# First batch's keys and queries loaded at once, scores of three pairs ahead of the first turning, transfers of one tile sent together

## The chip, the cores and the metric

One NeuronCore of a Trainium2 chip runs the whole program. The metric is the device time of one execution in microseconds (us), lower is better; the time of a kernel is the median of its runs. One further execution is taken by the hardware profiler, and all rows below are of that one.

## The reference

Inputs are random: `q`, `k`, `v` are (4 batches, 8 heads, 576 positions, 64), `s` is (4, 8, 576). All in fp32.

```python
scores = q @ k.T / 8
cum = cumsum(maximum(s, 0))
bias = -(cum[:, None] - cum[None, :])
scores = where(causal, -1e9, scores + minimum(bias, 0))
attn = softmax(scores)              # per batch and head
x = (attn @ v), heads side by side  # (4 * 576, 512)
x = ((x @ w_a) * (x @ w_b)) @ w_out          # w_a, w_b: 512 x 1536
h = x @ w_in                                 # w_in: 512 x 2048
out = (maximum(h, 0) + alpha * minimum(h, 0)) @ w_out2
```

## The kernel before

The 2304 tokens are worked in four blocks of the feed-forward part (`sizes`: 512, 512, 512 and 768 tokens). Each weight product is made of three fp32r products, since inputs and weights are split into a high part and a remainder (`wh`, `wl`; `xh`, `xl`; `gh`, `gl`). Blocks 0 to 2 run `ffn`, block 3 runs `ffn_seven`, which saves one of eight products. Weights come as 64-bit numbers, 90 tiles of 512 KB; in block 0 (and partly in block 1) each is decoded (`decode`: ScalarE, then VectorE) and stored once as fp32 in `w_d`, from which the later blocks read. `prefetch` loads weight tiles up to `ahead` tiles in front of the one in use.

Attention is cut per batch into the first 512 positions (`QA`) and the last 64 (`QB`), and into four pairs of heads (`HP`). For a pair: `load_kq` and `load_v` load, `s01` and `s23` make the scores of four strips of 128 queries (`q_k` on TensorE, then `soften`: minimum on VectorE, exponential on ScalarE, scaling on VectorE or GpSimd). In batch 0 `turn` then turns the probabilities on TensorE (twenty 128 x 128 products a pair, evicted into `pts`) and `av` multiplies with the values. In later batches the turning is done by VectorE in 32 x 32 tiles and by a way out to memory and back (`turned`: `zt`, `zd`, then `pt` or `pb`). The last 64 queries of a batch have steps of their own, `s4` and `av_b`, which need the tile `pb` (one buffer) and their own load of values with the argument `u = 1`: six pieces, a memset of a part of the tile ahead of them.

Only batch 0's attention stands ahead of the feed-forward part (`first_attention`, the first stage). The attention of later batches is cut into steps (`attention` lists them), which are strewn into the feed-forward blocks: `plan[0]` (batch 1) into block 0, `plan[1]` (batch 2 and the last queries of batch 1, then the last queries of batch 0 alone) into block 1, and so on.

The order of instructions on every engine is written by a planner (`Order`) while the program is built: a chain of work is a generator which yields the engines it could use with a cost, the planner takes whichever starts first, and `run.pe` advances its clock. A transfer is `dma`: a fixed cost on SP's queue, a transfer time by size, and an assumed time to land (`run.landing`, from `LANDING`, longer after the first stage). A chain with several `yield from dma(...)` issues the second one only after the planned landing of the first. `Slots` are counters of free buffers. Engines run their queues in order, SP too: a transfer that waits holds all behind it.

`due` takes the next step when its share of the block has come; outside block 0 it first asks `possible`, and puts the step off while its lag is below `BEHIND` (4) steps. `possible` looks at `s01`, `s23`, `s4` and `two_av`; any other step, `av_b` among them, counts as possible.

In `first_attention` before, the keys of pairs 0 and 1 are asked for at the start, those of pair i + 2 in round i, out of three buffers `kq`; scores of pair i + 1 follow a round behind the turning of pair i - 1; weights begin in round 2 (`FROM_WEIGHTS`), with ten ahead.

At the end, `store` copies each of the six output tiles of block 3 through four buffers `t` and sends it by SP.

Of the kernel before, what the change touches and what calls it, by code (L numbers as in the profile page):

```python
# [9 lines left out]
F32 = mybir.dt.float32  # L10
# [11 lines left out]
P = 128  # L22
D = 64
# [41 lines left out]

FROM_WEIGHTS, AHEAD, FROM_LEAD, FROM_STEPS, STEPS = 2, 10, 3, 4, 3

# [144 lines left out]
def attention_two_moe_kernel(  # L212
# [102 lines left out]
    def dma(o, i):  # L315
        yield {"sp": 480}, 700
        nc.sync.dma_start(o, i)
        yield {"dma": prod(o.shape) / (180 if o.dtype == U16 else 90)}, run.landing

    def split(src, hi, lo, sbuf=True):  # L320
        yield from copy(hi, src, 0.52 if sbuf else 1.04)
        yield from sub(lo, src, f32(hi), sbuf)


    def split_by(src, hi, lo, by):
# [14 lines left out]

    xh, xl = (
        [xp.tile([P, KD, 512], F32R, name=f"x{j}{i}") for i in range(2)] for j in "hl"
    )
    ovh = xp.tile([P, KD, OV], F32R, name="ovh")
# [39 lines left out]
    def running_sums(s_sb):  # L384
        nc.vector.tensor_scalar(s_sb, s_sb, 0.0, 8.0, op0=ALU.max, op1=ALU.mult)
        nc.vector.tensor_tensor_scan(cum[:, 0:S], s_sb, s_sb, 0.0, op0=ALU.add, op1=ALU.max)
        nc.sync.dma_start(cum_d, cum[:, 0:S])
        nc.vector.tensor_copy(cum[:, S:S + QB], cum[:, QA:S])
# [30 lines left out]

    def leave(b, t, o):  # L420
        if t < QA // P:
            yield from dma(out[b * S + t * P:b * S + (t + 1) * P, :], o)
        else:
            ends = [(2 * t - 2 * QA // P + j + 1) * S for j in range(2)]
            halves = [
                run.spawn(dma(out[e - QB:e, :], o[j * QB:(j + 1) * QB]), run.t)
                for j, e in enumerate(ends)
            ]
            for half in halves:
                yield half  # L430
        run.give(of_t, run.t)

# [18 lines left out]
    def load_v(b, hp, u):  # L451
        c0 = 2 * hp * D
        got = []

        def chain():
            yield of_vb
            vr = raw.tile([P, 5, 2 * D], F32, name="vb", tag="vb", bufs=VB)
            got.append(vr)
            if b + u >= TURN:
                keys = v[b, 0:QA, c0:c0 + 2 * D].rearrange("(c j k) d -> j k c d", j=4, k=32)  # L460
                if u:
                    yield {"pool": 240}, SEEN
                    nc.gpsimd.memset(vr[:, 4, :], 0.0)
                for j in range(4):
                    yield from dma(vr[j::4, 0:4, :], keys[j])
                    if u and j < 2:
                        k0 = QA + 32 * j
                        yield from dma(vr[j::4, 4, :], v[b, k0:k0 + 32, c0:c0 + 2 * D])
                return
            yield from dma(  # L470
                vr[:, 0:4, :], v[b, 0:QA, c0:c0 + 2 * D].rearrange("(c p) d -> p c d", p=P)
            )
            if u:
                yield {"pool": 240}, SEEN
                nc.gpsimd.memset(vr[QB:P, 4, :], 0.0)
                yield from dma(vr[0:QB, 4, :], v[b, QA:S, c0:c0 + 2 * D])

        v_t[b, hp, u] = got, run.spawn(chain(), slack=SL_QK)
# [20 lines left out]
    def load_kq(b, hp, u):  # L499

        got = []

        def chain():
            if not u and b >= STACK:
                halves = [run.spawn(stack(b, 2 * hp + j, got), run.t) for j in range(2)]
                yield halves[0]
                yield halves[1]
                return
            yield of_kq
            kq = raw.tile([P, 2 * QA], F32, name="kq", tag="kq", bufs=KQ)  # L510
            got.append(kq)
            if u:
                yield from dma(kq[:, 0:S + P], kq_b[b, hp])
            else:
                for j in range(2):
                    own = slice(j * D, (j + 1) * D)
                    yield from dma(kq[own], kq_a[b, 2 * hp + j, own])

        kq_t[b, hp, u] = got, run.spawn(chain())

    def load_sums(b, h, u):

        got = []

        def chain():
            yield of_c1 if u else of_c0
            nk = S if u else QA
            cb = raw.tile([P, nk], F32, name=f"cb{u}", tag=f"cb{u}", bufs=2 if u else CB)
            got.append(cb)
            n = P // (u + 1)  # L530
            for j in range(u + 1):
                bh = b * H + (u + 1) * h + j
                yield from dma(
                    cb[j * n:(j + 1) * n], cum_d[bh:bh + 1, 0:nk].to_broadcast([n, nk])
                )

        cb_t[b, h, u] = got, run.spawn(chain())

    def q_k(b, hp, r, dst):
# [30 lines left out]
        if r == 3:  # L570
            kq_t.pop((b, hp, 0))
            run.give(of_kq)

# [245 lines left out]

    def t4(b, hp, j):  # L820

        if j == 0:
            z_t[b, hp, 4] = probabilities(b, hp, 4)
        z = z_t[b, hp, 4]
        k, n = (QB, P) if j else (P, QA)
        at = slot()
        tp = banks[at][0:k, 0:n]
        for c in range(n // P):
            k0 = j * QA + c * P
            nc.tensor.transpose(tp[:, c * P:(c + 1) * P], z[:, k0:k0 + k], ident)  # L830
        run.pe(n / P * 107)
        if j:
            z_t.pop((b, hp, 4))
            run.give(of_z[4])

        def chain():
            if j == 0:
                yield of_pb
                pb_t[hp] = raw.tile([P, 5 * P], F32, name="pb", tag="pb")
                yield {"pool": 240}, SEEN  # L840
                nc.gpsimd.memset(pb_t[hp][QB:P, QA:5 * P], 0.0)
            o = j * QA
            yield from copy(pb_t[hp][0:k, o:o + n], tp, 1.04)

        e_t[b, hp, 4 + j] = read_by(at, chain())

    def av_b(b, hp):

        turned = b + 1 >= TURN
        if turned:  # L850
            settle((b, hp, 4))
        else:
            run.need(*(e_t.pop((b, hp, 4 + j)) for j in range(2)))
        got, ready = v_t.pop((b, hp, 1))
# [3 lines left out]
        pv = banks[at][:, 0:QB]  # L858
        for c in range(5 if turned else 0):
            for j in range(2):  # L860
# [3 lines left out]
                    p[:, 2 * j:2 * j + 2, c, :], start=c == 0, stop=c == 4,  # L864
                )
        for c in range(0 if turned else 5):
            for j in range(2):
                o = c * P + j * QB
                nc.tensor.matmul(
                    pv[64 * j:64 * j + 64], got[0][:, c, j * D:(j + 1) * D], pb[:, o:o + QB],  # L870
                    start=c == 0, stop=c == 4,
                )
# [13 lines left out]
    def first_attention():  # L886
# [6 lines left out]
        run.now = 2000.0  # L893
        run.pump()
        running_sums(s_sb)
        run.now = 5000.0
        for rs in ((0, 1), (2,)):
            both(0, 0, rs)
        for i in range(HP + 2):
            if i + 2 < HP:  # L900
                load_kq(0, i + 2, 0)
            if i < HP:
                load_v(0, i, 0)
                both(0, i, (3,))
                s01(0, i)
                if i + 1 < HP:
                    both(0, i + 1, (0, 1))
            if 0 <= i - 2:
                av(0, i - 2)
            if i < HP:  # L910
                s23(0, i, 2)
                if i + 1 < HP:
                    both(0, i + 1, (2,))
                s23(0, i, 3)
            if i == FROM_WEIGHTS:
                nc.sync.dma_start(alpha_sb, alpha)
                ahead = AHEAD
                prefetch()
            if i == FROM_LEAD:
                for f, args in plan[0][0]:  # L920
                    f(*args)
            if 0 <= i - 1 < HP:
                for c in range(3):
                    for j in range(2):
                        turn(0, 2 * (i - 1) + j, c)
            if i >= FROM_STEPS:
                for f, args in plan[0][1][:STEPS]:
                    f(*args)
                del plan[0][1][:STEPS]

# [303 lines left out]
    def possible(f, args):  # L1234
        rings = 1 if f == two_av else 2
        if f not in (s01, s23, s4, two_av):
            return True
        if not seen(*(reader[i] for i in ring[:rings] if i in reader)):
            return False
        if f == two_av:  # L1240
# [4 lines left out]
            )  # L1245
        b, hp = args[:2]
        if f == s4:
            return seen(kq_t[b, hp, 1][1], z_t[b, hp, 4][1])
# [170 lines left out]
    def ffn_seven(blk, sums):  # L1419
# [334 lines left out]
    def ffn(blk):  # L1754
# [57 lines left out]
        def store(t):  # L1812
            yield of_t
            o = ft.tile([P, DM], F32, name="o", tag="t")
            yield from copy(o, acc[t], 1.04, SHRUNK ** 2)
            run.spawn(leave(blk, t, o), run.t)

# [142 lines left out]
```

## Time and profile before

| | us |
|---|---|
| median of 3 runs | 991.97 |
| runs | 991.25 to 992.36 |
| the profiled execution: its time | 991.26 |
| the profiled execution: span from first to last instruction | 989.5 |

The profile shows one execution. A timeline row gives the start, the time of the (merged) instructions, engine, source line and operation, the number of instructions, and in brackets how long the engine had stood idle and who released it. A line is often that of a helper: L317 is `dma`, L292 `dve`, L276 `act`, L284 a copy by ScalarE. PE is TensorE, PEld its weight load, DVE VectorE, ACT ScalarE, POOL GpSimd, SPq the queue of SP. Matmuls overlap, so the distance of their starts, not their length, is their pace. PEclk is the granted clock of TensorE: 1.00 is 2.4 GHz, 0.50 is 1.2 GHz.

### The profile page before, as it was taken

The numbers are of one execution on the slowest core, as the hardware profiler recorded it, in microseconds if no ns is written. First come the engines' busy times: TensorE is split into PE (matmuls) and PEld (weight loads), VectorE is DVE, ScalarE is ACT, GpSimd is POOL, SyncE is SP. The second block draws the span as 40 slices with busy tenths as digits, with TensorE's granted clock in tenths as the row PEclk, the third lists the DMA queues.
The fourth block names the chain that finished last, engine by engine and source line by source line (L and its number), as shares of the span: only waits on it lengthen the run. The fifth ranks groups of instructions, "written<-read, shape, count | busy, mean of one in ns | idle before, by whom it ended". The sixth has DMA issues, their size and how long they took to land.

```text
span 989.5 us, 15862 instructions
## 1 busy us (share of the span) xinstructions
PE 964.1 (97%) x5235; PEld 811.8 (82%) x5235; DVE 745.3 (75%) x1725; ACT 559.3 (57%) x1162; POOL 231.9 (23%) x291
## 2 busy tenths in 40 slices
PE   6999999999999999969999999999999999999997
PEld 5577777788888888858888888888899999999896
DVE  7897878868788878847578868666497888788772
ACT  6976767657665657526455547544552333566443
POOL 2130113321155556303235434522100000000000
PEclk9999999999999999979999999999999999999999
DMA  7589997789599978977498786855403223021202
GB/s 191 179 283 320 344 364 248 280 291 320 202 285 297 319 247 280 283 222 231 151 273 252 214 273 195 252 177 176 161 24 105 65 64 103 27 65 65 64 0 65
DMA packets 140115, 196.78 MB, mean 199 GB/s; under 512 B 35776, under 2 KB 79808, under 8 KB 140032
## 3 DMA queue, kind: packets, MB, share of 16 engines
q1 hardware_dynamic: 130240, 177.93, 57.5%
q10 hardware_dynamic: 9792, 17.83, 4.9%
q8 instruction: 41, 0.67, 0.3%
q14 instruction: 42, 0.34, 0.1%
HBM read 152.13 MB, written 43.59 MB: 198 GB/s over the span
## 4 chain that ended last, share of the span: by engine, by line
PE 94%; DVE 2%; DMA 2%; ACT 2%; issue 0%; SPq 0%; ACTq 0%
PE bank L1223 21%; PE bank L1224 21%; PE bank L1225 21%; PE bank L1854 5%; PE bank L1856 4%; PE bank L1855 4%; PE bank L804 3%; PE bank L1707 2%; PE bank L1706 2%; PE bank L1708 2%; PE bank L547 2%; PE bank L744 1%; PE bank L566 1%; PE bank L862 1%; DMA kq<-in_kq_a_dram 1%; ACT z L276 1%
## 5 line engine op out<-in xcount | busy, mean ns | idle before, releaser
L1223 PE MATMUL bank<-xh,wh 128*128 128x512 f32 (+1 forms) x620 | 237.8, 384 | 0.0
L1224 PE MATMUL bank<-xl,wh 128*128 128x512 f32 (+1 forms) x620 | 234.3, 378 | 0.9 <-DVE xl L292 0.9
L1225 PE MATMUL bank<-xh,wl 128*128 128x512 f32 (+1 forms) x620 | 234.1, 378 | 0.0
L284 ACT ACTIVATE wh<-raw 128x512 fp32r<-128x512 f32 (+1 forms) x198 | 115.0, 592 | 91.8 <-PE bank L1224 39.0
L1223 PEld LDWEIGHTS bank<-xh,wh 128*128 128x128 f32 x620 | 116.5, 188 | 25.7 <-issue 6.5
L1224 PEld LDWEIGHTS bank<-xl,wh 128*128 128x128 f32 x620 | 116.6, 188 | 19.9 <-DVE xl L292 1.4
L1225 PEld LDWEIGHTS bank<-xh,wl 128*128 128x128 f32 x620 | 116.5, 188 | 19.4
L301 POOL TENSOR_TENSOR wl<-raw,wh 128x512 fp32r<-128x512 f32 x68 | 92.1, 1359 | 114.7 <-ACT wh L284 82.8
L301 DVE TENSOR_TENSOR wl<-raw,wh 128x512 fp32r<-128x512 f32 (+1 forms) x136 | 84.4, 633 | 39.9 <-ACT wh L284 33.6
L276 ACT ACTIVATE z<-z,mn 128x512 f32<-128x512 f32 (+4 forms) x144 | 83.0, 578 | 36.9 <-DVE mn L292 36.2
L1223 PE MATMUL bank<-gh,wh 128*128 128x512 f32 (+1 forms) x240 | 89.6, 373 | 0.0
L1224 PE MATMUL bank<-gl,wh 128*128 128x512 f32 (+1 forms) x240 | 88.6, 369 | 0.0
L1225 PE MATMUL bank<-gh,wl 128*128 128x512 f32 (+1 forms) x240 | 88.4, 368 | 0.0
L1854 PE MATMUL bank<-wh,gh 128*128 128x512 f32 x192 | 77.8, 405 | 0.0
L284 ACT ACTIVATE gh<-g 128x512 fp32r<-128x512 f32 x84 | 52.8, 628 | 43.1 <-DVE g L292 42.8
L1856 PE MATMUL bank<-wh,gl 128*128 128x512 f32 x192 | 75.5, 393 | 0.0
L1855 PE MATMUL bank<-wl,gh 128*128 128x512 f32 x192 | 75.5, 393 | 0.0
L1004 ACT ACTIVATE top<-raw 128x512 f16<-128x512 bf16 x90 | 69.2, 785 | 7.1 <-DMA raw<-in_w_dram 3.8
L301 DVE TENSOR_TENSOR gl<-g,gh 128x512 fp32r<-128x512 f32 x68 | 51.6, 759 | 18.4 <-ACT gh L284 17.5
L301 POOL TENSOR_TENSOR wl<-w,wh 128x512 fp32r<-128x512 f32 x24 | 31.8, 1323 | 134.8 <-ACT wh L284 92.0
L311 DVE TENSOR_SCALAR z<-z,sm 128x512 f32<-128x512 f32 (+4 forms) x103 | 59.0, 597 | 1.3
L292 DVE STREAM_TRANSPOSE zt<-z 128x384 f32<-128x384 f32 (+2 forms) x88 | 56.2, 650 | 4.8 <-DMA zd<-zt 3.8
(149 smaller groups left out, 1915.0 us busy)
## 6 DMA issues: line engine op xcount, KB each, us to landing
raw<-w_d SPq DMA_DIRECT2D x91, 512.0 KB, 4.3
raw<-in_w_dram SPq DMA_DIRECT2D x90, 512.0 KB, 5.9
w_d<-w ACTq DMA_DIRECT2D x46, 256.0 KB, 5.7
zd<-zt SPq DMA_DIRECT2D x48, 192.0 KB, 4.7
pt<-zd SPq DMA_DIRECT2D x48, 192.0 KB, 5.6
kq<-in_kq_a_dram SPq DMA_DIRECT2D x16, 512.0 KB, 6.1
vb<-in_v_dram SPq DMA_DIRECT2D x112, 64.0 KB, 4.4
zd<-zt SPq DMA_DIRECT2D x24, 256.0 KB, 2.9
```

What stands on the lines that cost most here:

```text
L276: nc.scalar.activation(o, i, func, **k)
L284: nc.scalar.activation(o, i, AF.Copy, scale=by)
L292: f(*args, **k)
L301: (nc.gpsimd if eng == "pool" else nc.vector).tensor_tensor(o, i0, i1, op=ALU.subtract)
L311: (nc.gpsimd if eng == "pool" else nc.vector).tensor_scalar(o, i, s0, s1, op0=ALU.mult, op1=ALU.mult)
L1004: nc.scalar.activation(top.bitcast(F16).rearrange("p (n t) -> p n t", t=2)[:, :, 1], r.bitcast(BF16)[:, 4:4 + 4 * WN].rearrange("p (n t) - ...
L1223: nc.tensor.matmul(o, wh, ih, start=first, stop=False)
L1224: nc.tensor.matmul(o, wh, il, start=False, stop=False)
L1225: nc.tensor.matmul(o, wl, ih, start=False, stop=last)
L1854: nc.tensor.matmul(acc[t], gh[:, c], wh, start=first, stop=False)
L1855: nc.tensor.matmul(acc[t], gh[:, c], wl, start=False, stop=False)
L1856: nc.tensor.matmul(acc[t], gl[:, c], wh, start=False, stop=last)
```

## The change

1. Keys and queries of batch 0 go into two tiles of two pairs each (`kq_0`), in the memory that the second block's `x` has later; all four pairs are asked for at the start, and their values too. Batch 0 takes none of the three `kq` buffers.
2. Two weight tiles (`EARLY_TILES`) are asked for between the keys of pairs 1 and 2; ten ahead from the scores of pair 1 on.
3. The order of the first stage is written out: scores of pairs 0, 1 and 2, turning of 0, scores of 3, then turnings and products with values in turn. The load for batch 1 (`lead`) comes after the scores of pair 1. The store of `cum_d` moves from the running sums to behind the scores of pair 0.
4. `dmas` starts several transfers of one tile at once, where a chain issued one behind the other: values of later batches (four or six pieces), halves of keys, the two halves of `cb`, and rows of the output.
5. `possible` knows `av_b`: it waits until the planner sees `pb` and the values.
6. In block 3, the two output tiles which are made first take buffers `d`, and the last tile is copied and sent in two halves, by ScalarE on its own queue and by VectorE on SP's.
7. Code for a way of turning that no batch takes (`t4`, branches in `av_b` and `load_v`) is removed.

```diff
-FROM_WEIGHTS, AHEAD, FROM_LEAD, FROM_STEPS, STEPS = 2, 10, 3, 4, 3
+AHEAD, EARLY_TILES, STEPS = 10, 2, 3
...
+    def dmas(*pairs):
+
+        sent = [run.spawn(dma(o, i), run.t) for o, i in pairs]
+        for c in sent:
+            yield c
...
-    xh, xl = (
-        [xp.tile([P, KD, 512], F32R, name=f"x{j}{i}") for i in range(2)] for j in "hl"
-    )
+    xh, xl = ([xp.tile([P, KD, 512], F32R, name=f"x{j}0")] for j in "hl")
+    kq_0 = [xp.tile([P, 2, 2 * QA], F32, name="kq", tag=f"x{j}1") for j in "hl"]
...
-        nc.sync.dma_start(cum_d, cum[:, 0:S])
...
+            if b + u < TURN:
+                yield from dma(
+                    vr[:, 0:4, :], v[b, 0:QA, c0:c0 + 2 * D].rearrange("(c p) d -> p c d", p=P)
+                )
                 return
-            yield from dma(
-                vr[:, 0:4, :], v[b, 0:QA, c0:c0 + 2 * D].rearrange("(c p) d -> p c d", p=P)
-            )
+            keys = v[b, 0:QA, c0:c0 + 2 * D].rearrange("(c j k) d -> j k c d", j=4, k=32)
+            pairs = [(vr[j::4, 0:4, :], keys[j]) for j in range(4)]
             if u:
                 yield {"pool": 240}, SEEN
-                nc.gpsimd.memset(vr[QB:P, 4, :], 0.0)
-                yield from dma(vr[0:QB, 4, :], v[b, QA:S, c0:c0 + 2 * D])
+                nc.gpsimd.memset(vr[:, 4, :], 0.0)
+                for j in range(2):
+                    k0 = QA + 32 * j
+                    pairs.append((vr[j::4, 4, :], v[b, k0:k0 + 32, c0:c0 + 2 * D]))
+            yield from dmas(*pairs)
...
-            yield of_kq
-            kq = raw.tile([P, 2 * QA], F32, name="kq", tag="kq", bufs=KQ)
+            if b or u:
+                yield of_kq
+                kq = raw.tile([P, 2 * QA], F32, name="kq", tag="kq", bufs=KQ)
+            else:
+                kq = kq_0[hp // 2][:, hp % 2]
             got.append(kq)
             if u:
                 yield from dma(kq[:, 0:S + P], kq_b[b, hp])
             else:
-                for j in range(2):
-                    own = slice(j * D, (j + 1) * D)
-                    yield from dma(kq[own], kq_a[b, 2 * hp + j, own])
+                own = [slice(j * D, (j + 1) * D) for j in range(2)]
+                yield from dmas(*((kq[o], kq_a[b, 2 * hp + j, o]) for j, o in enumerate(own)))
...
         run.now = 2000.0
         run.pump()
+        ahead = EARLY_TILES
+        prefetch()
+        run.now = 3000.0
+        run.pump()
+        for i in range(2, HP):
+            load_kq(0, i, 0)
+        for i in range(HP):
+            load_v(0, i, 0)
+        run.pump()
         running_sums(s_sb)
         run.now = 5000.0
...
+        scores(0)
+        nc.sync.dma_start(alpha_sb, alpha)
+        nc.sync.dma_start(cum_d, cum[0:BH, 0:S])
+        scores(1)
+        ahead = AHEAD
+        prefetch()
+        f, args = lead.pop(0)
+        f(*args)
+        scores(2)
+        turns(0)
+        scores(3)
+        for x, j in ((xh, "h"), (xl, "l")):
+            x.append(xp.tile([P, KD, 512], F32R, name=f"x{j}1", tag=f"x{j}1"))
+        for f, args in lead:
+            f(*args)
+        turns(1)
+        av(0, 0)
+        turns(2)
+        av(0, 1)
+        turns(3)
+        av(0, 2)
+        of_steps(STEPS)
+        av(0, 3)
+        of_steps(STEPS)
...
-        rings = 1 if f == two_av else 2
-        if f not in (s01, s23, s4, two_av):
+        rings = 1 if f in (two_av, av_b) else 2
+        if f not in (s01, s23, s4, two_av, av_b):
             return True
...
+        if f == av_b:
+            return (b, hp, 4) in e_t and seen(e_t[b, hp, 4], v_t[b, hp, 1][1])
...
         def store(t):
-            yield of_t
-            o = ft.tile([P, DM], F32, name="o", tag="t")
-            yield from copy(o, (acc + banks[0:2])[t], 1.04, SHRUNK ** 2)
-            run.spawn(leave(blk, t, o), run.t)
+            slots = of_t if t < QA // P else of_d
+            yield slots
+            if t < QA // P:
+                o = ft.tile([P, DM], F32, name="o", tag="t")
+            else:
+                o = pools["big"]([P, T], F32, "d", 5)[:, 0:DM]
+            src = (acc + banks[0:2])[t]
+            if t + 1 == QA // P:
+                for c in (slice(0, DM // 2), slice(DM // 2, DM)):
+                    run.spawn(last_half(t, o, src, c), run.t)
+                return
+            yield from copy(o, src, 1.04, SHRUNK ** 2)
+            run.spawn(leave(blk, t, o, slots), run.t)
+
+        def last_half(t, o, src, c):
+            by_act = c.start == 0
+            if by_act:
+                yield from act(o[:, c], src[:, c], AF.Copy, scale=SHRUNK ** 2)
+            else:
+                yield from dve(
+                    DM // 2, 1.04, nc.vector.tensor_scalar, o[:, c], src[:, c], SHRUNK ** 2, None,
+                    op0=ALU.mult,
+                )
+            rows = out[blk * S + t * P:blk * S + (t + 1) * P, c]
+            yield {"act" if by_act else "sp": 480}, 700
+            (nc.scalar if by_act else nc.sync).dma_start(rows, o[:, c])
```

In the new `first_attention`, `scores(i)` is `both` and then `s01`, `s23(2)`, `s23(3)` of pair i; `turns(i)` its six turnings; `of_steps(3)` the next three steps of `plan[0]`.

## Rows read from the trace of the kernel before

**Rows 1.** The page: busy us of each engine, its share of the span, instructions
```profile
...
PE 964.1 (97%) x5235; PEld 811.8 (82%) x5235; DVE 745.3 (75%) x1725; ACT 559.3 (57%) x1162; POOL 231.9 (23%) x291
...
```

**Rows 2.** Waits of TensorE: for whom, us in total, times, longest us
```profile
...
PE bank L862 <- DMA vb<-in_v_dram: 7.9, 1, 7.9
PE bank L399 <- DVE cum L386: 5.4, 1, 5.4
...
```

**Rows 3.** Busy us by stretch (columns: engines, granted clock, DMA share, GB/s)
```profile
...
0.00:54.34 54.34, 44.06 (x277) 30.31 (x277) 41.61 (x182) 42.94 (x129) 10.89 (x25) 0.97 0.67 185
...
62.00:190.00 128.00, 127.06 (x659) 100.28 (x659) 103.27 (x227) 88.03 (x167) 30.09 (x24) 1.00 0.92 314
...
```

**Rows 4.** Timeline of the start: start us, us, engine, line, operation
```profile
...
1.19 1.21 SPq L317 DMA_DIRECT2D kq<-in_kq_a_dram  x2
...
7.71 0.48 PE L560 MATMUL bank<-cums,rows 64*128 64x128 f32 x2
...
9.12 0.58 PE L566 MATMUL bank<-kq 64*128 64x128 f32 x1 [0.40 <-DMA kq<-in_kq_a_dram]
...
13.30 0.90 PE L560 MATMUL bank<-cums,rows 64*128 64x128 f32 x1
...
```

**Rows 5.** The chain that ended last, its start: start us, us, what
```profile
...
5.60 3.48 DMA kq<-in_kq_a_dram
...
```

**Rows 6.** Timeline of TensorE in the first stage
```profile
...
24.36 0.33 PE L560 MATMUL bank<-cums,rows 64*128 64x128 f32 x2
...
25.44 2.38 PE L811 MATMUL bank<-pt,vb 128*64 128x512 f32 x16
27.75 0.44 PE L560 MATMUL bank<-cums,rows 64*128 64x384 f32 x2
...
29.85 2.40 PE L771 MATMUL bank<-ident,z 128*128 128x128 f32 x20
...
```

**Rows 7.** Busy us by stretch of the first stage
```profile
...
0.00:7.70 7.70, 2.33 (x13) 2.31 (x13) 4.69 (x8) 4.87 (x20) 2.40 (x10) 1.00 0.47 110
...
17.13:24.36 7.23, 4.40 (x21) 3.80 (x20) 7.02 (x42) 6.58 (x21) 3.41 (x6) 0.76 1.05 311
...
30.00:38.00 8.00, 8.00 (x63) 5.24 (x63) 6.78 (x33) 8.00 (x25) 1.58 (x3) 1.00 0.00 0
...
```

**Rows 8.** Timeline of TensorE around the wait for values
```profile
...
416.50 0.80 PE L862 MATMUL bank<-pb,vb 128*64 128x64 f32 x20
...
434.66 1.33 PE L862 MATMUL bank<-pb,vb 128*64 128x64 f32 x20 [7.87 <-DMA vb<-in_v_dram]
...
440.68 0.39 PE L1225 MATMUL bank<-xh,wl 128*128 128x512 f32 x1
...
```

**Rows 9.** Busy us by stretch around the wait for values
```profile
...
436.00:438.00 2.00, 2.00 (x5) 1.62 (x6) 0.23 (x1) 0.23 (x1) 0.00 (x0) 0.50 0.34 79
...
```

**Rows 10.** Timeline of GpSimd and of SP in the same stretch
```profile
...
417.37 0.20 POOL L463 MEMSET vb<- 128x128 f32 x1 [2.17 <-PE bank L862]
...
424.12 0.58 SPq L317 DMA_DIRECT2D pb<-zd  x1
...
431.90 1.90 SPq L317 DMA_DIRECT2D vb<-in_v_dram  x3
...
```

**Rows 11.** Waits of SP from 405 to 436 us
```profile
...
SPq L317 <- DVE zt L292: 4.5, 2, 3.6
...
```

**Rows 12.** DMA issues from 400 to 436 us: KB each, median us to landing
```profile
...
vb<-in_v_dram SPq DMA_DIRECT2D x10, 64.0 KB, 4.4
...
pb<-zd SPq DMA_DIRECT2D x1, 320.0 KB, 5.5
...
```

**Rows 13.** Timeline of TensorE and of ScalarE at the end
```profile
...
982.77 0.39 PE L1708 MATMUL bank<-wh,gl 128*128 128x512 f32 x1
...
983.45 0.60 ACT L284 ACTIVATE o<-bank 128x512 f32<-128x512 f32 x1 [1.03 <-DMA out_dram<-o]
984.78 0.60 ACT L284 ACTIVATE o<-bank 128x512 f32<-128x512 f32 x1 [0.74 <-DMA out_dram<-o]
```

More of the change, by code (lines that the diff above doesn't have):

```diff
@@ L418, in attention_two_moe_kernel, with leave @@
     NB = len(sizes)
-    def leave(b, t, o):
+    def leave(b, t, o, slots):
         if t < QA // P:
@@ L424, in leave @@
             ends = [(2 * t - 2 * QA // P + j + 1) * S for j in range(2)]
[L425 to L431, printed above, removed]
+            yield from dmas(
+                *((out[e - QB:e, :], o[j * QB:(j + 1) * QB]) for j, e in enumerate(ends))
+            )
+        run.give(slots, run.t)
     pb_t, scores = {}, []
@@ L458, in chain @@
             got.append(vr)
[L459 to L468, printed above, removed]
+            if b + u < TURN:
+                yield from dma(
+                    vr[:, 0:4, :], v[b, 0:QA, c0:c0 + 2 * D].rearrange("(c p) d -> p c d", p=P)
+                )
                 return
-            yield from dma(
-                vr[:, 0:4, :], v[b, 0:QA, c0:c0 + 2 * D].rearrange("(c p) d -> p c d", p=P)
-            )
+            keys = v[b, 0:QA, c0:c0 + 2 * D].rearrange("(c j k) d -> j k c d", j=4, k=32)
+            pairs = [(vr[j::4, 0:4, :], keys[j]) for j in range(4)]
             if u:
                 yield {"pool": 240}, SEEN
-                nc.gpsimd.memset(vr[QB:P, 4, :], 0.0)
-                yield from dma(vr[0:QB, 4, :], v[b, QA:S, c0:c0 + 2 * D])
+                nc.gpsimd.memset(vr[:, 4, :], 0.0)
[3 more added lines that the diff above has]
+            yield from dmas(*pairs)
         v_t[b, hp, u] = got, run.spawn(chain(), slack=SL_QK)
@@ L530, in chain @@
             n = P // (u + 1)
[L531 to L534, printed above, removed]
-                )
+            yield from dmas(*(
+                (
+                    cb[j * n:(j + 1) * n],
+                    cum_d[bh:bh + 1, 0:nk].to_broadcast([n, nk]),
+                )
+                for j, bh in enumerate(range(b * H + (u + 1) * h, b * H + (u + 1) * (h + 1)))
+            ))
         cb_t[b, h, u] = got, run.spawn(chain())
@@ L571, in q_k @@
             kq_t.pop((b, hp, 0))
-            run.give(of_kq)
+            if b:
+                run.give(of_kq)
     def z_space(r, b, h):
@@ L818, in av @@
         x_done[b].append(read_by(at, split(pv, *parts, False)))
[L820 to L845, printed above, removed]
-    def av_b(b, hp):
[L849 to L853, printed above, removed]
+    def av_b(b, hp):
+        settle((b, hp, 4))
         got, ready = v_t.pop((b, hp, 1))
@@ L858, in av_b @@
         pv = banks[at][:, 0:QB]
-        for c in range(5 if turned else 0):
+        for c in range(5):
             for j in range(2):
@@ L864, in av_b @@
                     p[:, 2 * j:2 * j + 2, c, :], start=c == 0, stop=c == 4,
[L865 to L871, printed above, removed]
                 )
@@ L894, in first_attention @@
         run.pump()
+        ahead = EARLY_TILES
[7 more added lines that the diff above has]
+        run.pump()
         running_sums(s_sb)
         run.now = 5000.0
[L897 to L929, printed above, removed]
@@ new lines, in first_attention, with scores, turns, of_steps @@
+        lead, steps = plan[0]
+        def scores(i):
+            both(0, i, (0, 1))
+            both(0, i, (2,))
+            both(0, i, (3,))
+            s01(0, i)
+            s23(0, i, 2)
+            s23(0, i, 3)
+        def turns(i):
+            for c in range(3):
+                for j in range(2):
+                    turn(0, 2 * i + j, c)
+        def of_steps(n):
+            for f, args in steps[:n]:
+                f(*args)
+            del steps[:n]
+        scores(0)
+        nc.sync.dma_start(alpha_sb, alpha)
@@ new lines, in first_attention @@
+        nc.sync.dma_start(cum_d, cum[0:BH, 0:S])
[10 more added lines that the diff above has]
+        for f, args in lead:
+            f(*args)
+        turns(1)
[4 more added lines that the diff above has]
+        av(0, 2)
@@ L1648, in store @@
         def store(t):
-            yield of_t
-            o = ft.tile([P, DM], F32, name="o", tag="t")
-            yield from copy(o, (acc + banks[0:2])[t], 1.04, SHRUNK ** 2)
-            run.spawn(leave(blk, t, o), run.t)
+            slots = of_t if t < QA // P else of_d
[19 more added lines that the diff above has]
+                    op0=ALU.mult,
+                )
+            rows = out[blk * S + t * P:blk * S + (t + 1) * P, c]
+            yield {"act" if by_act else "sp": 480}, 700
+            (nc.scalar if by_act else nc.sync).dma_start(rows, o[:, c])
         def x2_part(o, j, d, c):
@@ L1815, in store @@
             yield from copy(o, acc[t], 1.04, SHRUNK ** 2)
-            run.spawn(leave(blk, t, o), run.t)
+            run.spawn(leave(blk, t, o, of_t), run.t)
         for f in range(NF1 + 1):
```

## Prediction

> **What bounds the kernel now.** I read the page first: TensorE is busy for 964.1 of 989.5 us [rows 1], so a gain can come only from the 25 us in which it stands still, from time at a low clock, or from stretches where its pipeline crawls. Next the waits of TensorE: two carry most, 7.9 us in one wait for a load of values and 5.4 us before its first instruction [rows 2]. Then the table by stretches: in the first stage, up to the first feed-forward product at 54.34, TensorE is busy for 44.1 us, so 10.3 are idle; from 62 to 190 us only 0.9 are [rows 3]. There and in most of the rest TensorE is the bound, so an earlier arrival at 54.34 is passed on, if the weights follow. The change touches the first stage, the place of the 7.9 us, and the end; I price each.
>
> **The first stage, its head.** Two chains lead to the first scores. The sums of `s` let the first score product run at 7.71; the change leaves this chain as it is. The keys and queries of pair 0: SP issues two halves at 1.19, then stands at the store of `cum_d`, which needs the scan, and issues the next only at 5.60, 3.48 us before TensorE goes on with it at 9.12, after 0.40 us of waiting [rows 4, 5]. In the new code all halves of pairs 0 and 1 precede the store. Pair 0 should be there by 1.8 + 3.5 = 5.3, ahead of 7.71, which frees about 1.4 us at the head. The later keys (1 MB), two weight tiles (1 MB) and the values (1 MB) are also sent early. The rows show 185 to 314 GB/s [rows 3]; at an assumed 230, pair 2, behind 2.5 MB, lands near 2 + 11 = 13 us, and it is wanted after two pairs of scores, near 14.5. I charge nothing; at 185 GB/s it would come at 15.5 and cost 1 us, which the range holds.
>
> **The first stage, its end.** Two bounds. TensorE's work at full speed: a pair's scores 1.08 + 2.10 = 3.18 us (24.36 to 25.44, 27.75 to 29.85), its twenty turnings 2.40, its values product 2.31 [rows 6]. Five pairs of scores (batch 1's first lies in the stage) and four of the others: 15.9 + 9.6 + 9.2 = 34.7. Pair 0's own scores were 2.0 us slower than 3.18 (7.71 to 13.30, less 0.40 [rows 4]), which I keep. 7.71 + 34.7 + 2.0 = 44.4 us: TensorE cannot be through earlier, a gain of 9.9. The other bound is ScalarE and VectorE, which share minima, exponentials, scaling, eviction and the weights' parts. From 7.7 to 54.34 they are busy for 38.1 and 36.9 us, 75.0 together, in 93.3; in the fullest stretches for 14.8 of 16.0 (30 to 38) and 13.6 of 14.5 us (17.13 to 24.36), 93% [rows 3, 7]. With all of it done at that density from 9.7 on (two us after the first product, as some scores must be there), it takes 40.3 us: 50.0. Part of the 75 belongs to weight tiles which the first products don't need yet; how much, the rows don't say, so I go some way from 50.0 towards 44.4: 48.8, a gain of **5.5**. The ends are 0 and 9.9. The new order speaks for a fuller ScalarE, since three pairs' scores are ahead of the first turning: now it is idle for 46.6 - 38.1 = 8.5 us. The clock of 0.76 from 17.13 to 24.36, behind TensorE's own 2.8 us of idle time there, costs 1.7 us [rows 7]; that it goes is part of the 5.5.
>
> Weights: block 0 runs almost without waits, at 314 GB/s [rows 3]. Two tiles are now decoded before the crush, so the stock at 48.8 should not be smaller than it is at 54.34. I cost this at nothing; what hides a late tile is that stock, and if the supply does not follow, this part falls to nothing.
>
> **The stall at 426.8.** It is the first `av_b` of batch 0's tail. TensorE stands for 7.87 us until 434.66. Then the clock is 0.50: the twenty small products take 1.33 us, where the same took 0.80 at 416.50, and from their end, 435.99, to 440.68 half of 4.7 us is lost. Price: 7.87 + 0.53 + 2.35 = 10.7 us [rows 8, 9]. What came last is a load of values: its pieces are issued one after another, each after the planner's landing of the one before, and the last three stand on SP at 431.90, behind a transfer that waited up to 3.6 us for a transposition [rows 10, 11]. Two edits attack it. `dmas` sends the six pieces in a row after the memset at 417.37: 6 x 0.6 = 3.6 us of SP, and landed by 421.2 + 4.4 = 425.6, before the stall begins. Left is `pb`: issued at 424.12, 5.5 us to land, 429.6 [rows 10, 12]. And `possible` now postpones `av_b` until the planner sees both; the lag may grow to four steps, a few us each by the distance of such steps, where 2.8 us are wanted. With both, **10.7**; with the first alone 7.87 - 2.8 = 5.1. What the change queues behind six pieces in a row is whatever SP issues next, a weight tile, up to 3.6 us later. Tiles are taken up to ten ahead, and one lasts for twelve products; I cost it at nothing, and rival 3 is what happens if that cover is gone.
>
> **The end.** The last product starts at 982.77 and takes 0.39. ScalarE's last two copies wait 1.03 and 0.74 us for buffers of outputs that are still leaving; the last ends at 985.38, and 4.1 us later all is over [rows 13]. In the new code two of the tiles use other buffers, so no copy waits, and the last is halved over two engines: 983.16 + about 0.4 = 983.6, then two sends side by side. Gain 985.4 - 983.6 = **1.8** us, with 4.1 kept; 1.2 to 2.2 if the halves take more or less than I assume. The Trainium skill (DMA: Bandwidth & Descriptors, Anatomy of one DMA) gives a transfer a fixed part of about 2.0 us and a part by bytes. By this half the bytes would land some 0.3 us earlier, an estimate, and the end would give 2.1. No row shows half a tile, so the sum stays at 1.8.
>
> **Sum.** 991.26 (the profiled execution: span 989.5 and 1.8 around it) - 5.5 - 10.7 - 1.8 = 973.3. The median of the runs lies 0.7 above the profiled one: **974.0**. A difference under 0.2% (2 us) could not be told from none.
>
> **Rivals.**
> 1. *The first stage gives nothing* (0.17). ScalarE is full from 30 to 38 us [rows 7]; if the early decodings stand in its order ahead of exponentials while their loads are still coming, or VectorE holds TensorE at each reuse of a bank, the stage ends near 54 again. Against it: 10.3 us of idle TensorE there. 991.97 - 10.7 - 1.8 - 0.5 = 979. One cause that would bring this about shows in the rows: idle time of 2.8 us goes with clock 0.76. The Trainium skill (TensorE: Matmul & The Clock Gate, A second HAM failure mode) says that small idle times between groups of products throttle the clock again; by that, three pairs of scores paced by VectorE would bring the low clock back.
> 2. *Half of the stall stays* (0.13): the planner takes `av_b` at once, and it waits for `pb` until 429.6. 991.97 - 5.5 - 5.1 - 1.8 = 979.6.
> 3. *Slower* (0.05): loads of values in a row on SP hold up the weights. There are 28 such loads, of four or six pieces. From 18.0 / 28 = 0.65 us of delay in each that comes through to TensorE, all is eaten; with 1 us it is 991.97 - 18.0 + 28 = 1002. Against it: 0.9 us of idle time in 128 [rows 3], so there is stock.
> 4. *TensorE bounds the first stage* (0.07): it ends at 44 to 45 us, and the time is 969.6.
>
> The forecast has 0.58, with 971 to 977. Half the stall and nothing from the first stage together give 984.6, about the upper end; the lower is the TensorE bound with the larger gain at the end, 969.2. Range **968 to 984**. Faster 0.93 (all but rival 3 and mishaps that add up), same 0.02, slower 0.05.
>
> **What would show it.** The first score product at 7.7 with no wait for keys after it; the first feed-forward product at 47 to 51; clock 1.00 from 17 to 25; no wait of TensorE over 1 us at the first lone `av_b` and clock 1.00 behind it; the last copy ending within 0.6 us of the last product. I am wrong if the first feed-forward product comes after 53, if a new wait of several us stands in blocks 0 to 2, or if TensorE waits for weights.

## The result, and the profile after

The changed kernel takes 996.96 us (median; 994.48 to 999.8) beside 991.9 us for the kernel before on the same chip: ratio 1.0052, 95% interval 1.0038 to 1.0065. It is slower by half a per cent, where I forecast 974.0 and gave slower a chance of 0.05.

The page of the changed kernel shows the span first; TensorE's busy time is that of [rows 1] to 0.1 us, so in sum the 3.1 us between the two spans are idle time of TensorE. The profiled execution, 994.48, is the fastest of the seven: 3.2 us of the 5.1 between the medians stand in the traces, the other 1.9 in none.

```profile
span 992.6 us, 15863 instructions
...
PE 964.0 (97%) x5235; PEld 810.5 (82%) x5235; DVE 739.1 (74%) x1711; ACT 560.5 (56%) x1169; POOL 236.5 (24%) x299
```

Its waits of TensorE (for whom, us in total, times, longest us) answer to [rows 2]:

```profile
PE bank L403 <- DVE cum L391: 5.4, 1, 5.4
PE bank L833 <- DMA pb<-zd: 5.0, 1, 5.0
PE bank L548 <- DVE mn L292: 3.0, 2, 1.9
PE bank L773 <- POOL z L311: 2.5, 4, 1.3
PE bank L806 <- DMA pt<-zd: 2.4, 2, 2.0
PE bank L548 <- DVE xl L301: 1.7, 1, 1.7
```

The 7.9 us for values are gone, and in their place stand waits for `pb`, for `pt` and for scores. Where they stand is read from the windows. The first two lines answer to [rows 3], the others bracket batch 0's tail, where [rows 8, 9] had the wait:

```profile
0.00:50.54 50.54, 41.05 (x277) 28.30 (x277) 40.85 (x178) 41.46 (x126) 12.22 (x26) 0.97 0.72 200
58.25:186.25 128.00, 127.05 (x659) 100.24 (x659) 102.15 (x228) 87.44 (x166) 30.74 (x24) 1.00 0.91 310
...
350.00:430.00 80.00, 72.23 (x445) 57.89 (x444) 56.66 (x133) 41.57 (x87) 34.51 (x46) 0.98 0.80 247
430.00:437.00 7.00, 7.00 (x48) 5.58 (x47) 5.49 (x12) 3.67 (x8) 1.38 (x2) 1.00 0.90 305
437.00:500.00 63.00, 57.96 (x294) 47.05 (x293) 36.49 (x68) 29.63 (x56) 14.44 (x20) 0.95 0.60 195
```

I set every feed-forward product of one trace against the same product of the other and read the lag (after minus before). It is -3.8 us at the first (50.54 instead of 54.34) and stays there for 300 us. From about 355 to 425 us it rises by 12.2 to +8.4. At the old stall it falls by 11.5 to -3.1. Between 465 and 474 it rises by 6.8 to +3.6, and the last product is 4.1 us late. Behind it 1.0 comes back, so the span is 3.1 us longer. The three gains of the forecast are there (3.8, 11.5 and 1.0 us); two losses in block 1, 12.2 and 6.8 us, eat them.

**The second loss, in full.** TensorE stands for `pb` and then runs at 0.50 of its clock, the lower of its two levels (its timeline, then the windows):

```profile
469.77 1.34 PE L833 MATMUL bank<-pb,vb 128*64 128x64 f32 x20 [5.04 <-DMA pb<-zd]
```

```profile
469.70:474.00 4.30, 4.23 (x27) 3.57 (x28) 1.57 (x3) 0.22 (x1) 0.00 (x0) 0.50 1.02 350
```

SP's timeline says why `pb` is late:

```profile
452.02 8.98 SPq L317 DMA_DIRECT2D vb<-in_v_dram  x4
461.05 1.24 SPq L317 DMA_DIRECT2D cb<-cum_d  x2
462.33 3.92 SPq L317 DMA_DIRECT2D vb<-in_v_dram  x6
466.30 0.58 SPq L317 DMA_DIRECT2D pb<-zd  x1
```

Ten pieces of values are ahead of `pb`. Six take 3.92 us, 0.65 each where I had reckoned 0.6. Four take 8.98. The chain through this stretch (start us, us, what) names what the longest stand was for:

```profile
450.67 9.07 DMA w_d<-raw
459.74 0.02 issue
459.76 0.60 SPq L317
...
466.30 3.12 DMA pb<-zd
...
469.77 1.34 PE bank L833 x20
```

A store of scaled weights, sent by ScalarE at 450.67, landed 9.07 us later, and SP's third piece of values, which had stood since 454.88, went at that moment. Of the 8.98 us, 4.9 are this stand, 1.4 an earlier one for a load of weights (landed at 454.24), and 2.6 the four issues. The piece has nothing to do with that store. The program's instructions, as they stand on SP, show the link: each transfer of SP and ScalarE signals one of eight semaphores, taken in turn, and first waits until the transfer that had it before has landed.

```
150 L317 DMA vb<-in_v_dram 32x4x128 [waits DMAHW7_49]
151 L317 DMA vb<-in_v_dram 32x4x128 [waits DMAHW0_49]
152 L317 DMA vb<-in_v_dram 32x4x128 [waits DMAHW1_49]
...
157 L317 DMA raw<-in_w_dram 128x2048 [waits DMAHW6_49,Activation_49]
158 L317 DMA raw<-in_w_dram 128x2048 [waits DMAHW7_49,Activation_49]
```

A small piece thus takes a place among eight as a tile of 512 KB does, and where the place is held by a slow transfer, SP stands with everything behind it. The Trainium skill (DMA: Bandwidth & Descriptors, Anatomy of one DMA) says that DMA engines don't wait on semaphores and that a wait is the issuing sequencer's, before dispatch; SP's stand of 4.9 us between two of its issues agrees.

**The first loss** begins with the same queue, with weights behind it. ScalarE's groups by line show how long it waited before `top`, the first step of decoding a tile; in the kernel before it was 3.8 us for loads in all:

```profile
L988 ACT ACTIVATE top<-raw 128x512 f16<-128x512 bf16 x90 | 68.7, 785 | 29.7 <-DMA raw<-in_w_dram 27.7 <-DVE w L292 1.5 <-ACT wh L284 0.5
```

SP's timeline there has six pieces between a load of `pb`, which itself had stood until a store of 6.35 us landed, and the next weight tile:

```profile
363.02 0.37 SPq L317 DMA_DIRECT2D pb<-zd  x1
363.44 0.50 SPq L317 DMA_DIRECT2D pt<-zd  x1
364.04 4.16 SPq L317 DMA_DIRECT2D vb<-in_v_dram  x6
...
368.94 0.45 SPq L317 DMA_DIRECT2D raw<-in_w_dram  x1
```

TensorE itself waits for no weight there. Of its 7.9 us of waits from 350 to 430 us, 4.7 are waits of score products (L548) for VectorE, 2.4 are for `pt` and 0.8 for parts of `g`. That the late tiles hold up VectorE is read from the order of the work; no run tries it alone. The last step of the climb, 3.7 of the 12.2 us, stands at a wait for `pt` of 2.0 us, and the chain to it is the way out to memory and back, with no stand on SP in it:

```profile
411.05 4.12 DMA zd<-zt
...
415.19 6.47 DMA pt<-zd
...
421.70 1.09 PE bank L806 x14
```

### The profile page after: what moved, and what is told of

Read it like the earlier page. It is cut to its first block, busy times and chain, and to the rows that moved or that the text cites. A ratio compares the mean times of both kernels' runs of the same rounds, so it can differ in the third digit from the quotient of the medians.

```text
span 992.6 us, 15863 instructions
## 1 busy us (share of the span) xinstructions
PE 964.0 (97%) x5235; PEld 810.5 (82%) x5235; DVE 739.1 (74%) x1711; ACT 560.5 (56%) x1169; POOL 236.5 (24%) x299
## 4 chain that ended last, share of the span: by engine, by line
PE 85%; DMA 6%; DVE 4%; SPq 1%; issue 1%; ACT 1%; DVEq 0%; ACTq 0%
PE bank L1207 19%; PE bank L1208 19%; PE bank L1209 19%; PE bank L1862 4%; PE bank L1863 4%; PE bank L1864 4%; PE bank L1715 2%; PE bank L1714 2%; PE bank L1716 2%; PE bank L806 2%; DMA zd<-zt 2%; PE bank L548 2%; PE bank L567 2%; DMA w_d<-raw 2%; SPq L317 1%; PE bank L746 1%
## 5 line engine op out<-in xcount | busy, mean ns | idle before, releaser
L301 POOL TENSOR_TENSOR wl<-raw,wh 128x512 fp32r<-128x512 f32 x74 | 98.9, 1339 | 103.9 <-ACT wh L284 91.2
L276 ACT ACTIVATE z<-z,mn 128x128 f32<-128x128 f32 (+4 forms) x144 | 82.7, 576 | 31.7 <-DVE mn L292 31.2
L988 ACT ACTIVATE top<-raw 128x512 f16<-128x512 bf16 x90 | 68.7, 785 | 29.7 <-DMA raw<-in_w_dram 27.7
L301 POOL TENSOR_TENSOR wl<-w,wh 128x512 fp32r<-128x512 f32 x27 | 36.3, 1347 | 129.9 <-ACT wh L284 80.6
```

Of the source, the lines that this page charges most:

```text
L276: nc.scalar.activation(o, i, func, **k)
L301: (nc.gpsimd if eng == "pool" else nc.vector).tensor_tensor(o, i0, i1, op=ALU.subtract)
L988: nc.scalar.activation(top.bitcast(F16).rearrange("p (n t) -> p n t", t=2)[:, :, 1], r.bitcast(BF16)[:, 4:4 + 4 * WN].rearrange("p (n t) - ...
```

## The experiments

Three theories first: A, the pieces sent in a row hold up what SP issues behind them (rival 3); B, postponing the lone `av_b` moves work to where it waits longer; C, the earlier start alone shifts the planner's order of block 1 into a worse one. The times:

| run | what it is | us | ratio to before, 95% interval |
|---|---|---|---|
| e1 | changed, values one piece after another | 981.87 | 0.9897 [0.9879, 0.9916] |
| e2 | changed, `av_b` not postponed | 998.0 | 1.0052 [1.0034, 1.0069] |
| e3 | before, `av_b` postponed | 980.81 | 0.9887 [0.9865, 0.9909] |
| e4 | before, values in a row | 1008.82 | 1.0169 [1.0147, 1.019] |
| e5 | changed, all later pieces one after another | 977.13 | 0.9854 [0.9838, 0.987] |
| e6 | changed, weight stores sent by GpSimd | 982.77 | 0.9908 [0.9889, 0.9927] |
| e7 | changed, four pieces of values merged | 981.52 | 0.9896 [0.9872, 0.992] |
| e8 | e5, `av_b` not postponed | 983.69 | 0.9924 [0.9902, 0.9945] |
| e9 | e7 with e5's order and e10's end | 981.52 | 0.9902 [0.9881, 0.9924] |
| e10 | e5, last tile of the output whole | 977.15 | 0.9856 [0.9839, 0.9873] |
| e11 | e5, no weight tile ahead of the scores | 973.0 | 0.9808 [0.9794, 0.9823] |

**e1.** In `load_v`:

```
-            yield from dmas(*pairs)
+            for j in range(4):
+                yield from dma(vr[j::4, 0:4, :], keys[j])
+                if u and j < 2:
+                    yield from dma(vr[j::4, 4, :], v[b, k0:k0 + 32, c0:c0 + 2 * D])
```

> The new kernel, but the pieces of a load of values are issued one after another again (all else of the change kept). Theory A (the pieces in a row fill SP's queue, and what stands behind them, pb and weight tiles, comes late: the new stalls of block 1): the stalls of 2.1 + 5.6 + 3.9 + 7.3 us in block 1 go for the most part, and the postponed av_b still removes the old one: 975 to 984. Theory B (the postponing of av_b moves later steps into each other): no change, 994 to 999. Theory C (the first stage's earlier end shifts all steps against the loads): no change, 994 to 999.

15 us come back. Up to the product at which the changed kernel's lag has climbed by 12.2 us, e1's climbs by 4.5. Of the step of 6.8 us behind 465, 0.8 is left, and the wait for `pb` shrinks from 5.0 to 0.8 (waits of TensorE in e1):

```profile
PE bank L548 <- DVE mn L292: 3.0, 2, 2.3
...
PE bank L833 <- DMA pb<-zd: 0.8, 1, 0.8
```

**e2.** `av_b` taken out of `possible`:

```
-        rings = 1 if f in (two_av, av_b) else 2
-        if f not in (s01, s23, s4, two_av, av_b):
+        rings = 1 if f == two_av else 2
+        if f not in (s01, s23, s4, two_av):
-        if f == av_b:
-            return (b, hp, 4) in e_t and seen(e_t[b, hp, 4], v_t[b, hp, 1][1])
```

> The new kernel, but av_b counts as possible at any time, as before the change. Theory A: the stalls of block 1 stay, and the first av_b may wait for pb as well: 994 to 1002. Theory B: the new stalls go, the old one is shortened by the pieces in a row: 980 to 988. Theory C: 994 to 1000.

No different from the changed kernel, so B falls: postponing doesn't cause the loss. Nor does the old stall return, as the pieces in a row are there in time.

**e3.** The same lines added to the kernel before, nothing else.

> The kernel before with only the edit of possible. Theory A: the stall of 10.7 us goes and nothing new comes: 980 to 984. Theory B: the old stall goes, but new ones come: 988 to 996. Theory C: as A, 980 to 984.

It is faster by 11.1 us, and the lag falls by 11 us at the old stall and nowhere else: the whole stall goes by this edit alone. Its first feed-forward product comes at 55.39, 1.0 us later than in the kernel before, though the edit touches nothing ahead of it: so much the first stage varies from one profile to another.

**e4.** `dmas` and its use in `load_v`, as in the change, in the kernel before.

> The kernel before with only the pieces of a load of values sent in a row. Theory A: the old stall is shortened by about 5, new ones of several us come in block 1: 991 to 1002. Theory B: 985 to 988, only the shorter stall. Theory C: 985 to 988.

Slower by 17 us, although the old stall goes here too. The lag climbs to 24 us at 419, in steps of 1 to 4 us all through blocks 0 and 1, and falls by 11.5 there. With neither the early start nor the postponing in it, A holds and C isn't needed. Its waits of TensorE show that the row holds up several kinds of loads, `pb`, `kq` and `pt` (lines one, two and four here) and work behind late weights:

```profile
PE bank L868 <- DMA pb<-zd: 3.6, 2, 2.0
PE bank L572 <- DMA kq<-in_kq_a_dram: 3.0, 2, 2.6
PE bank L1229 <- DVE g L292: 2.8, 2, 1.5
PE bank L810 <- DMA pt<-zd: 2.5, 2, 1.8
```

**e5.** e1, and the later halves of keys and queries and of broadcast sums in turn as well:

```
+                if b:
+                    for o, i in pairs:
+                        yield from dma(o, i)
+                else:
+                    yield from dmas(*pairs)
...
+            for j in range(u + 1):
+                bh = b * H + (u + 1) * h + j
+                yield from dma(
+                    cb[j * n:(j + 1) * n], cum_d[bh:bh + 1, 0:nk].to_broadcast([n, nk])
+                )
```

> The changed kernel with every load in pieces (values, later keys, broadcast sums) sent one piece after the landing of the other, as before; only the first batch's keys still go out together. The version with values alone in turn took 981.9, some 5 us more than 991.9 - 3.8 (first stage) - 11 (stall) - 1.0 (end) = 976. Theory D, the other groups in a row cost the 5 us as the values did, only less: 976, no loss left between 350 and 424 us. Theory E, the shifted plan of block 1 costs them: 982 and the losses stand where they stood.

977.1: D, some 4.7 us (by the two ratios 4.3). Of the waits for scores' banks 1.1 us are left of e1's 3.0. Of the climb of the lag 1.7 us are left (0.6 in e10, whose program differs at the last output tile alone). ScalarE's wait for weights before `top`, 27.7 us in the changed kernel, is 16.9 in e1 and 8.9 here.

**e6.** Values stay in a row; the slow store leaves the eight semaphores:

```
-            yield {"act": 330}, 700
-            nc.scalar.dma_start(w_d[i].bitcast(I32), source[0])
+            yield {"pool": 1000}, 700
+            nc.gpsimd.dma_start(w_d[i].bitcast(I32), source[0])
```

> The changed kernel, values in a row as they are, but the stores of scaled weights to DRAM are issued by GpSimd, with a semaphore of its own, instead of ScalarE. Theory F, pieces stand on SP because each of them waits for the landing of the eighth transfer before it, and the slow store is that one: the waits of 9 us among pieces go, at least 8 of the 15 us come back, 982 to 989, and the 5 us wait of TensorE at about 465 shrinks under 1.5. Theory G, it is the issuing time of six pieces on SP, or their bandwidth: 995 to 998, the wait at 465 stays.

982.8: F. SP still issues as many pieces (its timeline in e6), the six take as long as before, and the four no longer stand for 8.98 us:

```profile
446.49 3.49 SPq L317 DMA_DIRECT2D vb<-in_v_dram  x4
...
454.22 4.11 SPq L317 DMA_DIRECT2D vb<-in_v_dram  x6
```

The wait for `pb` is 2.0 us, a little over the 1.5 I had set. By the medians 14 us come back, by the two profiles 10.4. The second loss is 2.0 us here, but the first still climbs by 5.8 of the 12.2. So standing for the landing of stores is the larger part of the loss; whether the rest is the issue time of the pieces or stands for other landings isn't told apart. The edit also frees ScalarE's queue of the issues and loads GpSimd (the first feed-forward product gains only 2.5 us), so 14 is the sum of these.

**e7.** A second copy `vp` of the values' first 512 rows, in the turned order, in DRAM:

```
-            keys = v[b, 0:QA, c0:c0 + 2 * D].rearrange("(c j k) d -> j k c d", j=4, k=32)
-            pairs = [(vr[j::4, 0:4, :], keys[j]) for j in range(4)]
+            pairs = [(vr[:, 0:4, :], vp[b, :, c0:c0 + 2 * D].rearrange("(c p) d -> p c d", p=P))]
```

> The changed kernel with the four quarter pieces of each load of values merged in one transfer, from a second copy of the first 512 rows of values that lies in DRAM in the turned order; bytes and places on the chip are the same, and the loads still go out together with the two small pieces of the second kind. Theory F or G, the number of transfers in SP's order is the cost: 972 to 980, no wait of TensorE over 2 us between 350 and 470. Theory H, it is the early time at which the bytes of the values are asked for that takes the bandwidth from the weights: 990 to 998, as the changed kernel.

With the same bytes at the same early time, in 60 transfers instead of 144, 15 us come back and no wait for a load exceeds 1.0 us: the number of transfers in SP's order, not their bytes. It lies 1.5 us above the range that I gave for this; H falls.

**e8.** e5 with e2's lines.

> The first stage and the end of the change alone: all later pieces in turn, and the planner doesn't postpone the lone products with values. If the parts add up: 991.9 - 3.8 - 1.0 = 987, with the stall at about 423 as long as before (7 to 9 us). If starting 3.8 us earlier itself spoils block 1, 991 or more, with losses between 350 and 424.

The stall stands, with a wait of 6.0 us instead of 7.9; the first product is 3.2 us early and the end gives 1.0. In the profiled execution (986.09) these parts add up, within 1 us of the 987. The median of 983.69 is 3.3 us better than that sum, more than the shorter wait explains. C falls once more: the lag climbs by only 2.1 us from 350 to 420.

**e9.** e7's loads, e5's order, e10's end.

> Values merged as in the version that took 981.5, later keys and broadcast sums sent in turn as in the one that took 977.1, and the last tile of the output copied whole by ScalarE and sent by ScalarE. If merging and sending in turn cure the same queueing, there is nothing left to add but the end: 975 to 978, block 1 without losses over 1 us. If the merged loads cost by the time at which their bytes come (981.5 was slower than 977.1), 979 to 982.

The second case, 981.5: merged loads cost some 4 us more than pieces in turn (977.15 in e10, which differs in this alone), in a climb of the lag of 4.6 us from 355 to 420 us where e10 has 0.6, and not through TensorE waiting for them. What does it is left open.

**e10.** In `store`, for the last tile:

```
-                for c in (slice(0, DM // 2), slice(DM // 2, DM)):
-                    run.spawn(last_half(t, o, src, c), run.t)
+                yield from act(o, src, AF.Copy, scale=SHRUNK ** 2)
+                yield {"act": 480}, 700
+                nc.scalar.dma_start(out[blk * S + t * P:blk * S + (t + 1) * P, :], o)
```

> All later pieces in turn (977.1 before), and the last tile of the output not halved: copied whole by ScalarE, sent by ScalarE. In the halved form VectorE's half begins when ScalarE's is over, and its send waits behind three sends on SP. If that queue is what kept the end's gain at 1.0, the span ends 0.8 to 1.0 us earlier behind the last product, 4.5 us instead of 5.3, and the time is 976. If the landing of the outputs sent before it sets the end, nothing is gained.

Nothing gained. The last send is issued 1.0 us behind the last product and not 2.0, as wanted, yet the span ends 5.35 us behind it, 5.3 in e5. The second case: in the trace the last tile lands at 973.15, but the third of SP's outputs ahead of it, issued at 970.26, lands at 973.61, 4.26 us behind the last product. In e5 the half sent last lands 4.28 behind it. So the outputs ahead take back the 1.0.

**e11.** One constant:

```
-AHEAD, EARLY_TILES, STEPS = 10, 2, 3
+AHEAD, EARLY_TILES, STEPS = 10, 0, 3
```

> All later pieces in turn (977.1 before), and no weight tile asked for ahead of the scores; the rest of the first stage as changed. If the early decodings take ScalarE and VectorE from the exponentials, the first feed-forward product comes before 50.5, near 49. If they only fill idle time, it comes at 50.5 or later, and TensorE waits for weights in the first 10 us of block 0: 978 to 982.

The first feed-forward product comes 6.9 us earlier than before, at 47.45; in the eight profiles with two early tiles and ScalarE's stores it was 3.2 to 4.0 earlier. No wait for weights follows, the lag stays between -6.9 and -6.3 up to the old stall, and 973.0 us is 19 us below the kernel before and 24 below the changed one. The turnings of pair 0 show the place. First the changed kernel's timeline of TensorE, then e11's:

```profile
19.67 0.33 PE L773 MATMUL bank<-ident,z 128*128 128x128 f32 x1 [0.31 <-POOL z L311]
...
22.96 0.33 PE L773 MATMUL bank<-ident,z 128*128 128x128 f32 x1 [1.25 <-POOL z L311]
24.44 1.97 PE L773 MATMUL bank<-ident,z 128*128 128x128 f32 x8 [1.15 <-DVE z L311]
```

```profile
19.02 0.55 PE L776 MATMUL bank<-ident,z 128*128 128x128 f32 x3
21.21 2.31 PE L776 MATMUL bank<-ident,z 128*128 128x128 f32 x17 [1.64 <-POOL z L311]
```

Five waits, 3.7 us together (two of 0.69 and 0.26 are left out), become one of 1.6. (e5, from which e11 differs by the constant alone, has the same five, 3.5 us, each 1.0 us earlier.) Behind the five the clock is 0.50 for 2.6 us; in e11 it stays at 1.00 (windows of the changed kernel, then of e11):

```profile
17.13:24.36 7.23, 3.65 (x19) 1.93 (x17) 7.23 (x53) 6.91 (x26) 4.49 (x9) 0.97 1.08 334
24.44:27.00 2.56, 2.56 (x12) 2.56 (x13) 2.56 (x7) 2.28 (x7) 1.41 (x2) 0.50 0.39 83
```

```profile
17.13:24.36 7.23, 5.58 (x45) 4.15 (x43) 7.23 (x49) 7.23 (x25) 6.12 (x11) 1.00 0.99 368
```

That is 2.1 us of waits and about 1.3 of clock, against 3.1 gained in the first stage; the 4.1 between the times of e5 and e11 hold also the climb of 1.7 in e5, which is 0.4 here. By 24.44 GpSimd has issued 9 scalings in the changed kernel and 12 in e11; how the two tiles in the planner's order put the scalings back is argued, not shown.

## Why the prediction was wrong

**The step that failed** is the sentence on what is queued behind six pieces in a row: a weight tile, up to 3.6 us later, with stock to cover it, "I cost it at nothing". The runs gave it 15 us (e1), and 17 us net in the kernel before (e4), some 28 with the stall that it removes. Three things were wrong in it. It took 0.6 us for each piece, but a piece can stand until a place of eight is free, 4.9 us in the case above. It named a weight tile as what comes behind, but `pb`, `pt` and `kq` come behind too, and these have no stock. And it relied on a stock whose proof, under rival 3, was the 0.9 us of idle time in 128 [rows 3]. The changed kernel has no new idle time in that stretch either; but by the table of DMA issues (KB each, median us to landing) 8 pieces are sent in it, and 44 from 350 to 500 us, where the losses are:

```profile
vb<-in_v_dram SPq DMA_DIRECT2D x8, 64.0 KB, 4.8
```

```profile
vb<-in_v_dram SPq DMA_DIRECT2D x32, 64.0 KB, 3.6
vb<-in_v_dram SPq DMA_DIRECT2D x12, 16.0 KB, 2.0
```

The other groups sent in a row, later keys and broadcast sums, have no term in the sum at all; they cost another 4.7 us (e5).

**Rival 3** was what happened. It put the point of no gain at 0.65 us for each of 28 loads. The 15 us that the pieces of values cost (e1) are 0.54 each; the other groups in a row (4.7) and the early tiles (3.1) make up the rest of the 23 us between forecast and result. I gave it 0.05, on the evidence of a stretch in which its mechanism had hardly any occasion. It names weights; the runs show probabilities too.

**The stall** was right: 11.5 us went, 10.7 forecast. No wait stands at the first lone `av_b` (433.52), clock 1.00 from 430 to 437. That two edits were needed was wrong: e3 removes it by the postponing alone, and e2 by the row alone.

**The first stage** gave 3.8, not 5.5. The head came as forecast: scores at 7.70, no wait for keys. The bound from ScalarE and VectorE at 93%, 50.0, was nearly the measured 50.54, and the way from there towards 44.4 wasn't taken. What held it are the five waits for scaled probabilities and the low clock behind them, which go with the early tiles (e11). VectorE is busy for all of the 7.23 us there in both kernels, so that its time bounds that stretch is not excluded. Rival 1 was right in part, with 1.7 of the 5.5 missing. The clock of 1.00 that I wanted from 17 to 25 was 0.97, and 0.50 right behind. The rule of the Trainium skill that stood beside rival 1 (TensorE: Matmul & The Clock Gate, A second HAM failure mode) agrees: small idle times between groups, and the lower level behind, though at the turnings and not, as I had it, at the scores, which ran at 1.00 (7.70 to 17.13). The two early tiles, which I cost at nothing, cost 3.1 us; without them the stage gives 6.9.

**The end** gave 1.0, not 1.8 (1.2 to 2.2 forecast). The timeline of ScalarE, SP and VectorE after the last product (986.87 + 0.39), which answers to [rows 13]:

```profile
987.05 1.51 SPq L317 DMA_DIRECT2D out_dram<-o  x3
987.29 0.38 ACT L276 ACTIVATE o<-bank 128x256 f32<-128x256 f32 x1
987.71 0.37 ACTq L1660 DMA_DIRECT2D out_dram<-o  x1
987.71 0.42 DVE L292 TENSOR_SCALAR o<-bank 128x256 f32<-128x256 f32 x1 [8.07 <-ACT o L276]
988.65 0.61 SPq L1660 DMA_DIRECT2D out_dram<-o  x1
```

The halves follow one another, so the last copy ends 0.87 us behind the product and not within 0.6, and the last send goes out behind three others, so 4.5 us follow the copy, not 4.1. A whole tile sent 1.0 us earlier ends at the same time, since an output ahead of it lands last (e10). The halves landed 2.9 and 3.1 us after their issue, the two whole tiles sent last in e10 3.1 and 3.3, so half the bytes saved little, as the 0.3 us that the forecast left out of its sum had it.

With the failed step undone, e5 takes 977.1, and with the early tiles out too, e11 takes 973.0. That this is near 974.0 is in part luck: the three gains are 6.9, about 11 and 1.0 there, not 5.5, 10.7 and 1.8. What is left open: why merged loads lose 4 us to pieces in turn, what of the first loss remains in e6, and how the early tiles put the scalings back.

## What to carry to other kernels

Before sending small transfers together, look at what limits the number in flight (here eight, by the waits in the program's own list) and at what stands behind them on the same queue: each small one takes the place of a big one, and the queue stands until the transfer that holds the next place has landed, however slow. Evidence that there is stock is only good for the stretch where the new transfers will be. Work moved ahead of a tight start needs a price even when every engine has idle time there; two early tiles cost 3.1 us of the 6.9 that their stage could gain.

## What the hardware showed unexpectedly

A store of 256 KB, sent at 450.67, took 9.07 us to land, where its kind has a median of 5.1 in this kernel, and the loads that stood still for it had nothing to do with its data. And the lower level of the clock came behind the waits: over the five waits of pair 0's turnings the window reads 0.97, and the 2.56 us of products right behind them, without a wait, ran at 0.50.
